# Building the row tables of a two-pass edge sort with exclusive scans, padded differences and int32 quotients

## The chip, the cores and the metric

The kernel runs on one core of one Trainium2 chip. The metric is the device time of one execution in microseconds. In the text, PE is TensorE, DVE is VectorE, ACT is ScalarE, POOL is GpSimd and SP is SyncE, as the profile names them.

## The reference

A graph has 10,000 nodes with 64 channels of 4 components each, and 640,000 edges. Each edge has a source, a destination, four spherical harmonics `Y` and four features. Each edge makes a message out of its source's row, and the messages are summed by destination:

```python
N, deg, C, L, DE = 10000, 64, 64, 1, 4
E = N * deg

def reference(x, src, dst, Y, edge_feat, w_rad, cg, w_mix):
    R = _silu(edge_feat @ w_rad)                              # (E, C)
    xs = x[src]                                                 # (E, C, M)
    tp = jnp.einsum('eci,ef,ifo->eco', xs, Y, cg)             # (E, C, M)
    msg = R[:, :, None] * tp
    agg = _segment_sum(msg.reshape(-1, C * M), dst, N).reshape(N, C, M)
    return jnp.einsum('ncm,cd->ndm', agg, w_mix)
```

Sources and destinations are random integers.

## The kernel before

The kernel sorts the edges by destination in two passes through DRAM and then works on small buckets of destinations. The edges come in three parts (32, 37 and 31%), and each part goes through all steps.

**The first pass** (`pass1`) sends the edges of a part to 18 groups of 576 destinations. Edges lie in tiles of 128; 12 tiles make a chunk. For each chunk the kernel builds rows: a row holds up to 14 edges of one group, each packed into 10 words. A one-hot matmul (line 675) moves rows to their places on the partitions, ScalarE copies them out of PSUM (line 683, tile `rt`), and GpSimd writes 128 rows at a time to DRAM by an indirect DMA with an index tile (line 687, to `grp`).

**The second pass** (`pass2`) reads one group at a time and does the same for 18 buckets of 32 destinations, with rows of up to 15 edges (line 687, to `bkt`). In this pass a row that a chunk leaves half full is carried on to the next chunk (`carry`).

**The messages** (`messages`) are made bucket by bucket. GpSimd gathers the 1 KB rows of `x` for each tile of 128 edges by an indirect DMA (line 1030, tile `xg`, seven buffers, five buckets ahead of their use). TensorE and ScalarE make the radial factors, VectorE multiplies them in (line 1083), and TensorE sums by destination into `G` (line 1098). A gather can go out when line 1098 has read the buffer that it overwrites.

**The tables** (`tables`, what the change touches) are built before a pass can route: once for up to 24 (later 14) chunks of the first pass, and once for a group of the second pass, 83 times in all: 29 in the first pass, 54 in the second. A table works on small tiles of up to 64 partitions by 18 columns, one column for each group or bucket (`B` = 18) and one partition for each chunk:

- line 401 counts the edges of each chunk and bucket; line 404 copies the totals to `n`;
- `floor` (lines 374 and 375) divides by the row's size: one instruction multiplies, adds and writes int32, a second copies the int32 tile back to float32. It gives `R`, the rows that a chunk needs, in the second pass also `f` (whole rows ahead) and a rounded `tot`;
- lines 459 to 461 turn `R` into starts: an inclusive scan, minus `R`, and a copy of the last sum into a nineteenth column (`J` = 19);
- lines 468 to 475 give each tile's place inside its chunk (`at`, and its split into two bfloat16 parts `sb`);
- lines 480 to 487 give the distance from start to place in DRAM (`dl`) and its differences from column to column (`dd`): first column, middle, and last column by an instruction each. Lines 444 to 446 do the same for a limit in the second pass's last third (`final`);
- lines 492 to 500 spread `st`, `dd` and, in the second pass, a carried row's mark `go` along a diagonal for a matmul with ones; lines 517 to 555 compare with each partition's number and give the row numbers `dest`; lines 546 to 548 take them as integers and mark rows that overflow (`fl`);
- lines 568 to 575 rank the overflowing rows (an inclusive scan, minus itself) and write the index tile for line 687.

**The order.** In the first stage, part 0 of the first pass, a scheduler orders all engines but SP. After that the orders of PE, DVE and ACT are written out by the generators: `groups` calls the message steps one by one, and between them lets the first pass of the next part and the second pass take as many steps as their due times ask for. The steps of a table stand between the steps of routing and messages on the same DVE. POOL's queue holds the gathers and the stores of both passes in one order.

Of the kernel before, what the change touches and what calls it, by code (L numbers as in the profile page):

```python
# [18 lines left out]
F = mybir.dt.float32  # L19
# [6 lines left out]
P = 128  # L26
B = 18
# [52 lines left out]
class Kernel:  # L80
# [74 lines left out]
    def consts(self):  # L155
# [47 lines left out]
        for p in (self.p1, self.p2):  # L203

            p.on = c.tile([64, B * (p.T + 1)], F, name="on" + p.key)
            nc.vector.memset(p.on, 1.0)
            nc.vector.memset(p.on.rearrange("p (b t) -> p b t", b=B)[:, :, 0:1], 0.0)
            p.cols = c.tile([64, B * (p.T + 1)], F, name="cols" + p.key)
            nc.vector.memset(p.cols, 0.0)
        self.Ub = c.tile([P, P], BF, name="Ub")  # L210
        nc.vector.tensor_copy(self.Ub, self.U)
# [157 lines left out]

    def floor(self, out, x, r, up, nm, n):  # L370

        nc = self.nc
        t = self.ph.tile([P, B], I32, name="ri", tag="ri" + nm, bufs=1)
        nc.vector.tensor_scalar(t[:n], x, 1.0 / r, ((r - 0.5) if up else 0.5) / r - 0.5, op0=OP.mult, op1=OP.add)
        nc.vector.tensor_copy(out, t[:n])

    def tables(self, ps, D, nt, rows, kov, base, cap, final=False):
# [24 lines left out]
        sums = sums[:H].rearrange("p (b t) -> p b t", b=B)  # L402
        n = w("n", B)
        nc.vector.tensor_copy(n[:H], sums[:, :, T])
# [18 lines left out]
        if ps.carry:  # L423

            f, part = w("f", B), w("part", B)
            self.floor(f[:H], pre[:H], r, False, ps.key, H)
            nc.vector.scalar_tensor_tensor(part[:H], f[:H], -float(r), pre[:H], op0=OP.mult, op1=OP.add)
            nc.vector.tensor_tensor(n[:H], n[:H], pre[:H], op=OP.add)
            self.floor(R[:H], n[:H], r, True, ps.key, H)
            nc.vector.tensor_tensor(R[:H], R[:H], f[:H], op=OP.subtract)  # L430
            self.floor(tot[:H], tot[:H], r, True, ps.key, H)
            end, sh = w("end", B), w("sh", B)
            of = lambda t, a, n=H: t[:n].rearrange("p (m a) -> p m a", a=2)[:, :, a]
            nc.vector.tensor_tensor(end[:H], off[:H], tot[:H], op=OP.add)
            till = of(end, 1)
            if final:

                lim, dlim = w("lim", B), w("dlim", J)
# [19 lines left out]
        inc, st = w("inc", B), w("st", J)  # L458
        nc.vector.tensor_tensor_scan(inc[:H], self.ones[:H, :B], R[:H], 0.0, op0=OP.mult, op1=OP.add)
        nc.vector.tensor_tensor(st[:H, :B], inc[:H], R[:H], op=OP.subtract)  # L460
        nc.vector.tensor_copy(st[:N, B:], inc[:N, B - 1:])
        if ps.carry:
            nc.vector.tensor_tensor(self.most[:N], self.most[:N], inc[:N, B - 1:], op=OP.max)

        first = w("first", B)
        at = wk.tile([P, XW], F, name="at", tag="x1" + ps.key, bufs=1)[:, :T * B]
        if ps.carry:
            nc.vector.scalar_tensor_tensor(first[:H], st[:H, :B], float(r), part[:H], op0=OP.mult, op1=OP.add)
        else:
            nc.vector.tensor_scalar(first[:H], st[:H, :B], float(r), None, op0=OP.mult)  # L470
        nc.vector.tensor_tensor(at[:H].rearrange("p (t b) -> p b t", b=B), sums[:, :, :T],
                                first[:H].unsqueeze(2).to_broadcast([H, B, T]), op=OP.add)
        sb = wk.tile([H, T * B], BF, name="sb", tag="sb" + ps.key, bufs=3)
# [3 lines left out]

        dl, dd = w("dl", B), w("dd", J)
        if final:
            nc.vector.tensor_tensor(dl[:N], off[:N], base[:N], op=OP.add)  # L480
        else:
            nc.vector.tensor_tensor(dl[:N], cap[:N], off[:N], op=OP.min)
            nc.vector.tensor_tensor(dl[:N], dl[:N], base[:N], op=OP.add)
        nc.vector.tensor_tensor(dl[:N], dl[:N], st[:N, :B], op=OP.subtract)
        nc.vector.tensor_copy(dd[:N, 0:1], dl[:N, 0:1])
        nc.vector.tensor_tensor(dd[:N, 1:B], dl[:N, 1:], dl[:N, :B - 1], op=OP.subtract)
        nc.vector.tensor_scalar(dd[:N, B:], dl[:N, B - 1:], -1.0, float(ps.none), op0=OP.mult, op1=OP.add)
        eye = self.ident[:N, :N].unsqueeze(2).to_broadcast([N, N, J])
# [5 lines left out]
        if ps.carry:  # L494

            go, bq = w("go", J), w("bq", NC * J, NC, d=BF)
            nc.vector.memset(go[:N, 0:1], 0.0)
            nc.vector.tensor_scalar(go[:N, 1:], st[:N, :B], -2.0 * P, None, op0=OP.add)
# [40 lines left out]
        nc.vector.tensor_reduce(dest[:, :N], sts[:, :N * J].rearrange("p (c j) -> p c j", j=J), axis=AX.X, op=OP.add)  # L539
        nc.vector.tensor_scalar(dest[:, :N], dest[:, :N], self.pid, None, op0=OP.add)  # L540

        if final:
            nc.vector.tensor_tensor(fl[:, :N], dest[:, :N], lm[:, :N], op=OP.is_ge)
        else:
            di = w("di", NC, d=I32)
            nc.vector.tensor_copy(di[:, :N], dest[:, :N])
            nc.vector.tensor_scalar(di[:, :N], di[:, :N], ps.stride - 1, None, op0=OP.bitwise_and)
            nc.vector.tensor_scalar(fl[:, :N], di[:, :N], float(ps.cap), None, op0=OP.is_ge)
        if ps.carry:
# [3 lines left out]
            nc.vector.tensor_tensor(fl[:, :N], fl[:, :N], un[:, :N], op=OP.is_gt)  # L553
            nc.vector.scalar_tensor_tensor(dest[:, :N], un[:, :N], float(ps.none), dest[:, :N], op0=OP.mult, op1=OP.add)
            nc.vector.tensor_scalar(tg[:, :N], tg[:, :N], 2.0 * P, None, op0=OP.add)
# [6 lines left out]
        yield  # L562
        ov, rk = w("ov", 64), w("rk", NC)
# [5 lines left out]
        nc.vector.tensor_tensor(kov, kov, rk[0:1, N - 1:N], op=OP.add)  # L569
        nc.vector.tensor_tensor(rk[:, :N], rk[:, :N], ov[:, 32:32 + N], op=OP.subtract)  # L570
        nc.vector.tensor_tensor(rk[:, :N], rk[:, :N], ov[:, :N], op=OP.add)
        nc.vector.scalar_tensor_tensor(rk[:, :N], rk[:, :N], float(ps.ovf), dest[:, :N], op0=OP.add, op1=OP.subtract)
        nc.vector.tensor_tensor(rk[:, :N], rk[:, :N], fl[:, :N], op=OP.mult)
        idx = w("idx", NC, b=3, d=I32)
        nc.vector.tensor_tensor(idx[:, :N], rk[:, :N], dest[:, :N], op=OP.add)
        self.tab[ps.key] = (sb, idx, N, tg if ps.carry else None)
# [1023 lines left out]
```

## Time and profile before

| | before |
|---|---|
| runs, us | 8428.72, 8426.91, 8418.68 |
| median, us | 8426.91 |
| profiled execution, us | 8430.4 |
| its span, us | 8428.6 |
| granted TensorE clock, mean | 0.855 |
| DVE busy, us (share of the span) | 7181.2 (85%) |
| POOL busy, us (share) | 5881.9 (70%) |
| PE busy, us (share) | 5985.1 (71%) |
| ACT busy, us (share) | 4614.3 (55%) |
| gathers of `x` (line 1030) | 5165, 957 ns each |
| stores of sorted rows (line 687) | 417 + 489, 1008 ns each |

The span reaches from the first to the last instruction of one execution. Busy time of an engine leaves out the issuing of DMAs, so for POOL, which issues indirect DMAs from first to last, the short idle time between two of them has to be counted with them. A view by stretches gives the busy time of each engine between two moments; a view of waits gives who waited for whom, how long in total, how often, and the longest.

### The profile page before, as it was taken

The page shows a single profiled execution, that of the slowest core. Times are in us where ns is not written, and L with a number is a line of the kernel's source. Part 1 is how long each engine was busy: PE and PEld are TensorE (multiplying, and loading weights), DVE is VectorE, ACT ScalarE, POOL GpSimd, SP SyncE. Part 2 cuts the span into 40 slices and gives each one's busy share as a digit, 9 for nine tenths or more (in the row PEclk, how much of TensorE's full clock was granted, in tenths as well). Part 3 has the DMA queues.
Part 4 walks back from the last instruction along what each step waited for, and adds up shares of the span by engine and source line. Part 5 has one row for each costly group of instructions (what it writes and reads, how often), then busy time and mean ns, then how long its engine had stood idle before and what let it go on. Part 6 is the DMA issues. An engine that isn't in the chain of part 4 may idle for free. (4 is left out here: it accounts for less than half of the span.)

```text
span 8428.6 us, 133579 instructions
## 1 busy us (share of the span) xinstructions
PE 5985.1 (71%) x41164; PEld 4943.4 (59%) x41164; DVE 7181.2 (85%) x14990; ACT 4614.3 (55%) x12740; POOL 5881.9 (70%) x6113
## 2 busy tenths in 40 slices
PE   5666776777767767776676676766677777778776
PEld 3334655656555656565565565555566666666666
DVE  8988999999999889988898898867787888878775
ACT  5876666666666746655565565653443443434321
POOL 1226676777767767777777777777777777777776
PEclk8977888888888879888888888887898989888888
DMA  5313343443434434444444444444455555555543
GB/s 185 112 59 96 113 117 107 118 116 112 118 110 120 119 112 129 121 122 123 120 122 124 120 119 125 116 120 121 133 147 145 145 146 145 146 148 143 146 139 114
DMA packets 691501, 1051.54 MB, mean 125 GB/s; under 512 B 268789, under 2 KB 499107, under 8 KB 690792
## 3 DMA queue, kind: packets, MB, share of 16 engines
q0 software_dynamic: 285888, 732.64, 30.5%
q1 hardware_dynamic: 402312, 301.08, 12.1%
q10 hardware_dynamic: 2592, 9.19, 0.3%
q8 instruction: 345, 5.65, 0.3%
q14 instruction: 364, 2.98, 0.1%
HBM read 841.86 MB, written 215.89 MB: 125 GB/s over the span
## 5 line engine op out<-in xcount | busy, mean ns | idle before, releaser
L1030 POOL DMA_INDIRECT xg<-in_x_dram,sidx x5165 | 4940.6, 957 | 1750.4 <-issue 1345.0
L1098 PE MATMUL G<-S,xg 128*128 128x128 f32 x20660 | 2989.8, 310 | 158.2 <-ACT Gp L1127 129.4
L1098 PEld LDWEIGHTS G<-S,xg 128*128 128x128 f32 x20660 | 2837.7, 222 | 202.2 <-ACT Gp L1127 153.3
L675 PE MATMUL pr<-X,oh 128*128 128x300 bf16 (+1 forms) x10573 | 1668.3, 312 | 548.5 <-DVE oh L657 411.4
L1083 DVE TENSOR_TENSOR xg<-xg,pre 128x1536 f32<-128x1536 f32 (+1 forms) x939 | 1516.4, 1615 | 540.3 <-DMA xg<-in_x_dram,sidx 303.3
L665 ACT ACTIVATE sq<-i,rowf 128x128 f32<-128x128 f32 x6132 | 1882.1, 391 | 11.2 <-DVE rowf L626 7.3
L641 DVE TENSOR_TENSOR X<-dv,Wt 128x1800 f32<-128x1800 f32 (+4 forms) x906 | 1741.6, 1922 | 62.1 <-PE pr L675 10.4
L675 PEld LDWEIGHTS <-oh 128*128 128x128 bf16 x10573 | 1080.1, 105 | 983.1 <-DVE oh L657 483.7
L666 ACT ACTIVATE oh<-sq,ones 128x1024 bf16<-128x1024 f32 (+3 forms) x906 | 967.1, 1067 | 27.1
L1069 DVE TENSOR_TENSOR S<-dv,pay 128x768 f32<-128x768 f32 (+1 forms) x939 | 836.7, 891 | 87.3 <-PE G L1098 29.8
L1043 PE MATMUL pre<-identb,e 128*108 128x128 bf16 x1878 | 291.2, 241 | 867.5 <-DVE xg L1083 866.6
L1043 PEld LDWEIGHTS <-e 128*108 128x108 bf16 x1878 | 236.8, 140 | 1041.1 <-issue 792.3
L1059 ACT ACTIVATE pre<-pre 128x384 f32<-128x384 f32 (+1 forms) x939 | 426.6, 454 | 716.3 <-PE pre L1056 551.0
L687 POOL DMA_INDIRECT grp<-rt,idx x417 | 420.2, 1008 | 529.0 <-ACT rt L683 196.9
L1127 ACT ACTIVATE Gp<-G 128x256 f32<-128x256 f32 x626 | 238.6, 381 | 892.0 <-PE G L1098 647.3
L687 POOL DMA_INDIRECT bkt<-rt,idx x489 | 492.7, 1008 | 224.7 <-issue 112.4
L1048 ACT ACTIVATE sT<-pre 108x256 bf16<-108x256 f32 x939 | 353.2, 376 | 527.1 <-PE pre L1043 525.2
L1143 PE MATMUL po<-wf,Gs 128*128 128x256 f32 (+2 forms) x1392 | 390.8, 443 | 184.6 <-DVE Gs L1125 184.6
L683 ACT ACTIVATE rt<-pr 128x300 bf16<-128x300 f32 (+1 forms) x906 | 358.7, 396 | 278.6 <-PE pr L678 118.5
L1143 PEld LDWEIGHTS po<-wf,Gs 128*128 128x128 f32 (+2 forms) x1392 | 282.5, 209 | 278.1 <-DVE Gs L1125 181.7
L657 DVE TENSOR_TENSOR oh<-dv,pair 128x640 bf16<-128x640 bf16 (+2 forms) x869 | 420.6, 488 | 0.3
L609 ACT ACTIVATE pc<-pp 128x432 f32<-128x432 f32 (+3 forms) x471 | 236.3, 502 | 295.5 <-DVE pos L618 227.5
(286 smaller groups left out, 6086.1 us busy)
## 6 DMA issues: line engine op xcount, KB each, us to landing
xg<-in_x_dram,sidx POOLq DMA_INDIRECT x5165
sums<-Gp SPq DMA_DIRECT2D x626, 128.0 KB
old<-sums SPq DMA_DIRECT2D x313, 256.0 KB
bkt<-z SPq DMA_DIRECT2D x26, 990.0 KB
pay<-bkt SPq DMA_DIRECT2D x68, 225.0 KB
grp<-z SPq DMA_DIRECT2D x17, 590.0 KB
Wt<-grp SPq DMA_DIRECT2D x17, 590.0 KB
ye<-in_Y_dram SPq DMA_DIRECT2D x103, 96.0 KB
```

The lines of the kernel that those rows point to most:

```text
L641: nc.vector.tensor_tensor(X[:, :m, :].rearrange("p t (s w) -> p t s w", w=W), msk.unsqueeze(3).to_broadcast([P, m, ps.r, W]), QD[c // Q][1 ...
L665: nc.scalar.activation(sq[:, u, :], self.i128, AF.Square, bias=to, scale=-1.0)
L666: nc.scalar.activation(oh[:, v:v + len(at), :], sq[:, :len(at), :], AF.Relu, bias=self.ones[:, 0:1], scale=-2.0)
L675: nc.tensor.matmul(pr[:, :2 * ps.rw], oh[:, u, :], X[:, u, :].bitcast(BF), start=(u == 0), stop=(not on and u == m - 1))
L687: st = nc.gpsimd.indirect_dma_start(out=ps.dst, out_offset=bass.IndirectOffsetOnAxis(ap=idx[:, i:i + 1], axis=0), in_=RT.pop(c), in_offset ...
L1030: nc.gpsimd.indirect_dma_start(out=xg[:, t, :], out_offset=None, in_=self.x, in_offset=bass.IndirectOffsetOnAxis(ap=si[:, u:u + 1], axis=0))
L1043: nc.tensor.matmul(pre[:KR, 256 + 128 * h:384 + 128 * h], e[:, 36 * t:36 * t + KR], self.identb, start=True, stop=True)
L1059: nc.scalar.activation(RT[k], RT[k], AF.Silu)
L1069: nc.vector.tensor_tensor(S[:, :ut], self.eq[:, :ut].unsqueeze(3).to_broadcast([P, ut, NB, 4]), pb[:, :, 1:5].unsqueeze(2).to_broadcast([P ...
L1083: nc.vector.tensor_tensor(V, V, R.unsqueeze(3).to_broadcast([P, ut, 64, 4]), op=OP.mult)
L1098: nc.tensor.matmul(G[:, h].rearrange("p n f -> p (n f)"), v[:, 32 * h:32 * h + 32, :].rearrange("p c i -> p (c i)"), s.rearrange("p n f -> ...
L1143: nc.tensor.matmul(po[:nn, :256], Gs[:, h, f].rearrange("p b n -> p (b n)")[:, :nn], self.wf[:, h, f, :], start=(h + f == 0), stop=(h + f ...
```

## The change

The tables are built with fewer instructions on DVE; the values stay the same.

- `floor` writes the int32 tile and stops there. Where a quotient is read by the next computation, that reads int32 (`f`, `Ri`, `all`); only the first pass copies it to float32, since a matmul reads it.
- The totals are no longer copied to `n`: the strided view `sums[:, :, T]` is read in place, by the matmuls too.
- Some tiles are kept for the whole program with fixed outer columns that are set once at the start: `Rx` has a zero ahead of `R`, so that an inclusive scan over 19 columns gives the exclusive starts and the total in one instruction; `dlx` and `limx` have a zero ahead and the closing value behind, so that one subtraction of shifted views gives all 19 differences; `gone` has its zero column; `ov` has a zero in column 31, ahead of the counts in columns 32 and on, so that the rank scan starts one column early and is exclusive.
- In the first pass the product `first` goes into the addition that makes `at`; in the second, outside its last third, the minimum with a constant and the addition of the base are one instruction.
- `dest` plus the partition's number is written as int32 (`di`), and the later steps read that.
- Eleven memsets at the start set the fixed columns.

```diff
@@ consts
+            p.Rx = c.tile([64, B + 1], F, name="Rx" + p.key)
+            nc.vector.memset(p.Rx, 0.0)
+            p.dlx = c.tile([32, B + 2], F, name="dlx" + p.key)
+            nc.vector.memset(p.dlx, 0.0)
+            nc.vector.memset(p.dlx[:, B + 1:], float(p.none))
+            p.ov = c.tile([P, 64], F, name="ov" + p.key)
+            nc.vector.memset(p.ov, 0.0)
...
@@ floor
-        t = self.ph.tile([P, B], I32, name="ri", tag="ri" + nm, bufs=1)
-        nc.vector.tensor_scalar(t[:n], x, 1.0 / r, ((r - 0.5) if up else 0.5) / r - 0.5, op0=OP.mult, op1=OP.add)
-        nc.vector.tensor_copy(out, t[:n])
+        self.nc.vector.tensor_scalar(t, x, 1.0 / r, ((r - 0.5) if up else 0.5) / r - 0.5, op0=OP.mult, op1=OP.add)
@@ tables
-        n = w("n", B)
-        nc.vector.tensor_copy(n[:H], sums[:, :, T])
-        R = w("R", B)
+        Ri, R = w("Ri", B, d=I32), ps.Rx[:, 1:]
         if not ps.carry:
-            self.floor(R[:H], n[:H], r, True, ps.key, H)
+            self.floor(Ri[:H], sums[:, :, T], r, True)
+            nc.vector.tensor_copy(R, Ri[:H])
...
-        cn = n if ps.carry else R
+        cn = sums[:, :, T] if ps.carry else R
...
-            self.floor(f[:H], pre[:H], r, False, ps.key, H)
+            self.floor(f[:H], pre[:H], r, False)
             nc.vector.scalar_tensor_tensor(part[:H], f[:H], -float(r), pre[:H], op0=OP.mult, op1=OP.add)
-            nc.vector.tensor_tensor(n[:H], n[:H], pre[:H], op=OP.add)
-            self.floor(R[:H], n[:H], r, True, ps.key, H)
-            nc.vector.tensor_tensor(R[:H], R[:H], f[:H], op=OP.subtract)
-            self.floor(tot[:H], tot[:H], r, True, ps.key, H)
+            nc.vector.tensor_tensor(n[:H], sums[:, :, T], pre[:H], op=OP.add)
+            self.floor(Ri[:H], n[:H], r, True)
+            nc.vector.tensor_tensor(R, Ri[:H], f[:H], op=OP.subtract)
+            self.floor(all[:H], tot[:H], r, True)
...
-                nc.vector.tensor_copy(dlim[0:1, 0:1], lim[0:1, 0:1])
-                nc.vector.tensor_tensor(dlim[0:1, 1:B], lim[0:1, 1:], lim[0:1, :B - 1], op=OP.subtract)
-                nc.vector.tensor_scalar(dlim[0:1, B:], lim[0:1, B - 1:], -1.0, 4.0 * ps.none, op0=OP.mult, op1=OP.add)
+                nc.vector.tensor_tensor(dlim[0:1], self.limx[:, 1:], self.limx[:, :J], op=OP.subtract)
...
-        nc.vector.tensor_tensor_scan(inc[:H], self.ones[:H, :B], R[:H], 0.0, op0=OP.mult, op1=OP.add)
-        nc.vector.tensor_tensor(st[:H, :B], inc[:H], R[:H], op=OP.subtract)
-        nc.vector.tensor_copy(st[:N, B:], inc[:N, B - 1:])
+        nc.vector.tensor_tensor_scan(st[:H], self.ones[:H, :J], ps.Rx, 0.0, op0=OP.mult, op1=OP.add)
...
-        else:
-            nc.vector.tensor_scalar(first[:H], st[:H, :B], float(r), None, op0=OP.mult)
-        nc.vector.tensor_tensor(at[:H].rearrange("p (t b) -> p b t", b=B), sums[:, :, :T],
-                                first[:H].unsqueeze(2).to_broadcast([H, B, T]), op=OP.add)
+        nc.vector.scalar_tensor_tensor(at[:H].rearrange("p (t b) -> p b t", b=B),
+                                       first[:H, :B].unsqueeze(2).to_broadcast([H, B, T]), k, sums[:, :, :T],
+                                       op0=OP.mult, op1=OP.add)
...
+        elif ps.carry:
+            nc.vector.scalar_tensor_tensor(dl[:N], off[:N], float(ps.cap), base[:N], op0=OP.min, op1=OP.add)
...
-        nc.vector.tensor_copy(dd[:N, 0:1], dl[:N, 0:1])
-        nc.vector.tensor_tensor(dd[:N, 1:B], dl[:N, 1:], dl[:N, :B - 1], op=OP.subtract)
-        nc.vector.tensor_scalar(dd[:N, B:], dl[:N, B - 1:], -1.0, float(ps.none), op0=OP.mult, op1=OP.add)
+        nc.vector.tensor_tensor(dd[:N], ps.dlx[:N, 1:], ps.dlx[:N, :J], op=OP.subtract)
...
-            nc.vector.memset(go[:N, 0:1], 0.0)
...
-        nc.vector.tensor_scalar(dest[:, :N], dest[:, :N], self.pid, None, op0=OP.add)
+        di = w("di", NC, d=I32)
+        nc.vector.tensor_scalar(di[:, :N], dest[:, :N], self.pid, None, op0=OP.add)
...
-            nc.vector.tensor_copy(di[:, :N], dest[:, :N])
...
-        nc.vector.tensor_tensor_scan(rk[:, :N], self.ones[:, :N], ov[:, 32:32 + N], 0.0, op0=OP.mult, op1=OP.add)
+        nc.vector.tensor_tensor_scan(rk[:, :N + 1], self.ones[:, :N + 1], ov[:, 31:32 + N], 0.0, op0=OP.mult, op1=OP.add)
...
-        nc.vector.tensor_tensor(rk[:, :N], rk[:, :N], ov[:, 32:32 + N], op=OP.subtract)
```

In the order of DVE's instructions, here is the start of a table of the second pass between two routing steps, before (the rows are line, operation, output from inputs, and shape; the scan is listed as a fused operation in such rows):

```order
L374 TENSOR_SCALAR ri<-pre 64x18
L375 CAST f<-ri 64x18
L427 SCALAR_TENSOR_TENSOR part<-f,pre 64x18
L428 TENSOR_TENSOR n<-n,pre 64x18
L374 TENSOR_SCALAR ri<-n 64x18
L375 CAST R<-ri 64x18
L430 TENSOR_TENSOR R<-R,f 64x18
L374 TENSOR_SCALAR ri<-tot 64x18
L375 CAST tot<-ri 64x18
L434 TENSOR_TENSOR end<-off,tot 64x18
```

The same piece of DVE's order with the change:

```order
L384 TENSOR_SCALAR f<-pre 64x18
L435 SCALAR_TENSOR_TENSOR part<-f,pre 64x18
L436 TENSOR_TENSOR n<-sums,pre 64x18
L384 TENSOR_SCALAR Ri<-n 64x18
L438 TENSOR_TENSOR Rxbkt<-Ri,f 64x18
L384 TENSOR_SCALAR all<-tot 64x18
L443 TENSOR_TENSOR end<-off,all 64x18
```

The three casts are gone and the rest keeps its order. Further down in the same table on DVE, the distances and their differences, before:

```order
L482 TENSOR_TENSOR dl<-bc,off 9x18
L483 TENSOR_TENSOR dl<-dl,base 9x18
L484 TENSOR_TENSOR dl<-dl,st 9x18
L485 COPY dd<-dl 9x1
L486 TENSOR_TENSOR dd<-dl 9x17
L487 TENSOR_SCALAR dd<-dl 9x1
L492 TENSOR_TENSOR bs<-ident,st 9x171
```

And with the change:

```order
L487 SCALAR_TENSOR_TENSOR dlxbkt<-off,base 9x18
L491 TENSOR_TENSOR dlxbkt<-dlxbkt,st 9x18
L492 TENSOR_TENSOR dd<-dlxbkt 9x19
L497 TENSOR_TENSOR bs<-ident,st 9x171
```

Seven rows became four. In all, DVE's order has 14842 rows before and 13972 with the change. Behind the first stage the orders of PE, DVE and ACT are the same but for the rows that are left out. In the first stage, where the scheduler sets the order, some packing steps and matmuls stand some places earlier or later. POOL's queue has a store and a few gathers exchanged in a handful of places.

More of the change, by code (lines that the diff above doesn't have):

```diff
@@ L209, in consts @@
             nc.vector.memset(p.cols, 0.0)
+            p.Rx = c.tile([64, B + 1], F, name="Rx" + p.key)
[5 more added lines that the diff above has]
+            nc.vector.memset(p.ov, 0.0)
+        self.limx = c.tile([1, B + 2], F, name="limx")
+        nc.vector.memset(self.limx, 0.0)
+        nc.vector.memset(self.limx[:, B + 1:], 4.0 * self.p2.none)
+        self.gone = c.tile([32, B + 1], F, name="gone")
+        nc.vector.memset(self.gone, 0.0)
         self.Ub = c.tile([P, P], BF, name="Ub")
@@ L368, in digits, with floor @@
             yield
-    def floor(self, out, x, r, up, nm, n):
-        nc = self.nc
-        t = self.ph.tile([P, B], I32, name="ri", tag="ri" + nm, bufs=1)
-        nc.vector.tensor_scalar(t[:n], x, 1.0 / r, ((r - 0.5) if up else 0.5) / r - 0.5, op0=OP.mult, op1=OP.add)
-        nc.vector.tensor_copy(out, t[:n])
+    def floor(self, t, x, r, up):
+        self.nc.vector.tensor_scalar(t, x, 1.0 / r, ((r - 0.5) if up else 0.5) / r - 0.5, op0=OP.mult, op1=OP.add)
     def tables(self, ps, D, nt, rows, kov, base, cap, final=False):
@@ L423, in tables @@
         if ps.carry:
-            f, part = w("f", B), w("part", B)
-            self.floor(f[:H], pre[:H], r, False, ps.key, H)
+            f, part, n, all = w("f", B, d=I32), w("part", B), w("n", B), w("all", B, d=I32)
+            self.floor(f[:H], pre[:H], r, False)
             nc.vector.scalar_tensor_tensor(part[:H], f[:H], -float(r), pre[:H], op0=OP.mult, op1=OP.add)
-            nc.vector.tensor_tensor(n[:H], n[:H], pre[:H], op=OP.add)
-            self.floor(R[:H], n[:H], r, True, ps.key, H)
-            nc.vector.tensor_tensor(R[:H], R[:H], f[:H], op=OP.subtract)
-            self.floor(tot[:H], tot[:H], r, True, ps.key, H)
+            nc.vector.tensor_tensor(n[:H], sums[:, :, T], pre[:H], op=OP.add)
+            self.floor(Ri[:H], n[:H], r, True)
+            nc.vector.tensor_tensor(R, Ri[:H], f[:H], op=OP.subtract)
+            self.floor(all[:H], tot[:H], r, True)
+            tot = all
             end, sh = w("end", B), w("sh", B)
@@ L553, in tables @@
             nc.vector.tensor_tensor(fl[:, :N], fl[:, :N], un[:, :N], op=OP.is_gt)
-            nc.vector.scalar_tensor_tensor(dest[:, :N], un[:, :N], float(ps.none), dest[:, :N], op0=OP.mult, op1=OP.add)
+            nc.vector.scalar_tensor_tensor(dest[:, :N], un[:, :N], float(ps.none), di[:, :N], op0=OP.mult, op1=OP.add)
+            di = dest
             nc.vector.tensor_scalar(tg[:, :N], tg[:, :N], 2.0 * P, None, op0=OP.add)
```

29 lines of the change are left out of this document (15 added, 14 removed).

## The prediction

> **What bounds the kernel now.** I read the busy line of the page first, then the busy time by stage, then the waits of GpSimd and of VectorE in those stages, and last the order of time around the place where GpSimd waits for the last time.
>
> ```profile
> span 8428.6 us, 133579 instructions
> PE 5985.1 (71%) x41164; PEld 4943.4 (59%) x41164; DVE 7181.2 (85%) x14990; ACT 4614.3 (55%) x12740; POOL 5881.9 (70%) x6113
> ```
>
> VectorE (DVE) has the largest share, and the change takes work from VectorE alone. But a share over the whole span mixes stages. The stages, cut at the first gather (636 us) and at the last wait of GpSimd that I find further down (3288 us):
>
> ```profile
> core 0: us, PE busy (x) PEld busy (x) DVE busy (x) ACT busy (x) POOL busy (x), PEclk, DMA share, GB/s
> 0.00:636.00 636.00, 373.69 (x2155) 221.53 (x2156) 582.64 (x1594) 462.58 (x1248) 142.76 (x156) 0.85 0.35 118
> 636.00:3288.00 2652.00, 1877.30 (x12954) 1530.35 (x12953) 2418.08 (x5133) 1707.72 (x4787) 1861.98 (x1928) 0.84 0.40 114
> 3288.00:8300.00 5012.00, 3662.50 (x25597) 3126.95 (x25595) 4123.67 (x8168) 2430.26 (x6670) 3805.53 (x3956) 0.86 0.46 132
> ```
>
> GpSimd's busy time hides a fixed step between its indirect DMAs, which the order of time shows (columns: start, duration, what, idle before it and what ended that):
>
> ```profile
> 3288.22 0.96 POOL L1030 DMA_INDIRECT xg<-in_x_dram,sidx  x1 [1.13 <-PE G L1098]
> 3289.49 0.95 POOL L1030 DMA_INDIRECT xg<-in_x_dram,sidx  x1 [0.31 <-issue]
> ```
>
> Each indirect DMA costs its 0.96 us and then some 0.305 us in which the engine waits for nothing. From 3288 to 8300 us that gives 3805.5 + 3956 x 0.305 = 5012 us, which is the whole stretch: GpSimd issues without a pause for five of the eight milliseconds, and no work saved on VectorE there can move the end. From 636 to 3288 us the same sum is 1862.0 + 1928 x 0.305 = 2450 of 2652 us, so 202 us are true waiting. What GpSimd waits for there, and what it waits for behind it:
>
> ```profile
> engine line waited for: us in total, times, longest us
> POOL xg L1030 <- PE G L1098: 117.3, 45, 10.4
> POOL xg L1030 <- PE pre L1056: 57.0, 36, 5.4
> POOL bkt L687 <- ACT rt L683: 29.7, 14, 8.2
> ...
> POOL xg L1030 <- PE G L1098: 6.7, 15, 1.6
> ```
>
> The first three rows are 636 to 3288 us, the last one, with no single wait over 1.6 us, 3288 to 8300. Up to 3288 us a gather waits until the sums (line 1098) have read the tile it will overwrite; those sums wait for VectorE's products, and VectorE itself has few waits in the same stretch:
>
> ```profile
> DVE xg L1083 <- ACT pre L1059: 22.1, 17, 3.2
> DVE xg L1083 <- DMA xg<-in_x_dram,sidx: 17.2, 8, 4.5
> ```
>
> So: VectorE paces the first 3288 us, GpSimd's queue the rest, and the time is (moment of GpSimd's last real wait) + (its remaining work at 1.27 us a piece). Only VectorE time saved before 3288 us counts.
>
> **The change part by part.** The price of a removed instruction is not its duration but the step to the start of the next one, since independent instructions overlap. One table of the second pass, in order of time:
>
> ```profile
> 1250.03 0.17 DVE L404 COPY n<-sums 64x18 f32<-64x18 f32 x1
> 1250.12 0.34 DVE L638 TENSOR_TENSOR dv<-dv,slot 128x180 f32<-128x180 f32 x1
> ...
> 1263.97 0.17 DVE L375 CAST f<-ri 64x18 f32<-64x18 int32 x1
> 1264.17 0.17 DVE L427 SCALAR_TENSOR_TENSOR part<-f,pre 64x18 f32<-64x18 f32 x1
> ...
> 1266.86 0.17 DVE L460 TENSOR_TENSOR st<-inc,R 64x18 f32<-64x18 f32 x1
> 1266.96 0.13 DVE L461 COPY st<-inc 9x1 f32<-9x1 f32 x1
> 1267.02 0.14 DVE L463 TENSOR_TENSOR most<-most,inc 9x1 f32<-9x1 f32 x1
> ...
> 1275.65 0.17 DVE L483 TENSOR_TENSOR dl<-dl,base 9x18 f32<-9x18 f32 x1
> 1275.85 0.17 DVE L484 TENSOR_TENSOR dl<-dl,st 9x18 f32<-9x18 f32 x1
> 1276.05 0.14 DVE L485 COPY dd<-dl 9x1 f32<-9x1 f32 x1
> 1276.12 0.15 DVE L486 TENSOR_TENSOR dd<-dl 9x17 f32<-9x17 f32 x1
> 1276.20 0.13 DVE L487 TENSOR_SCALAR dd<-dl 9x1 f32<-9x1 f32 x1
> 1276.27 0.32 DVE L492 TENSOR_TENSOR bs<-ident,st 9x171 bf16<-9x171 f32 x1
> ...
> 1296.52 0.17 DVE L546 CAST di<-dest 128x9 int32<-128x9 f32 x1
> 1296.73 0.17 DVE L547 TENSOR_SCALAR di<-di 128x9 int32<-128x9 int32 x1
> ```
>
> Steps of what goes in a table of the second pass: the copy of n 0.09 us; three casts behind the divisions at 0.20, 0.60; the subtraction and the copy that made the scan exclusive (lines 460 and 461) 0.10 + 0.06 = 0.16; the separate addition of the base (483) 0.20; two of the three pieces of the difference (485 and 487) 0.07 + 0.07 = 0.14; the cast of the row number (546) 0.21; the subtraction behind the rank scan (570), which the next instruction waits for as it does for the casts, 0.20. The memset of line 497 I count at nothing, since the addition beside it covers it. Sum **1.60 us** of a table's VectorE time, for 12 instructions. The last third of the second pass keeps 483 and 546 as they are but loses the same two pieces of difference once more for its limits: 1.60 - 0.20 - 0.21 + 0.14 = 1.33 us. A table of the first pass loses the copy of n (0.20, since the division waits for it), 0.16, 0.14, 0.21, 0.20, and the product that made `first` (line 470, 0.20 like the casts of that shape, since the next one waits for it): **1.11 us** for 8 instructions.
>
> The upper bound of these prices is a whole duration and the 0.03 us of idle time that stand between a cast and its reader. For the 12 instructions that is 12 durations of 0.06 to 0.17, 1.8 us, and 12 x 0.03, so 2.2 us a table, and for the 8 of the first pass 1.5 us. The rows with independent neighbours are against it: line 463 starts 0.06 us after line 461 did, which takes 0.13. The Trainium skill, "VectorE: DVE Perf Modes", section "The DRAIN you can't avoid", has the stricter rule: the next operation does not start until the pipeline of the one before is empty, so each instruction costs its whole length and their count is what is to be cut; by it a table is worth 2.2 us and not 1.6. The trace disagrees with that for the 0.06 us step, and agrees where the next instruction reads the result.
>
> What is put in their place costs nothing that I can see: the scan runs over 19 instead of 18 columns, the rank scan over one more, the difference is one instruction over 19 instead of 17 columns. New forms are integer operands and a fused operation in the place of a plain one, and the first two rows, of one size, show a fused operation on integers at the price of a plain one on floats:
>
> ```profile
> L1066 DVE TENSOR_TENSOR dv<-dv,dlc 128x192 f32<-128x192 f32 x470 | 170.6, 363 | 8.5
> L794 DVE SCALAR_TENSOR_TENSOR Wt<-ye,pkh 128x192 int32<-128x192 int32 x206 | 67.8, 362 | 2.4
> L471 DVE TENSOR_TENSOR at<-sums,first 64x216 f32<-64x216 f32 x83 | 42.8, 516 | 2.6
> L497 DVE MEMSET go<- 9x1 f32 (+3 forms) x54 | 3.2, 59 | 0.0
> ```
>
> No row shows a fused operation that mixes a broadcast with a strided operand as the new line 471 does; its bounds are 516 ns as now, and twice that, 0.5 us lost a table. I take no loss, going by those two rows. Eleven memsets come in at the start, 59 ns each as line 497: 0.7 us.
>
> How many tables lie where it counts, by the busy time of two lines in the three stretches (line 460 runs once in every table, line 497 once in every table of the second pass):
>
> ```profile
> 0.00:636.00 636.00, 1.46 (x9) 0.85 0.35 118
> 636.00:3288.00 2652.00, 5.79 (x34) 0.84 0.40 114
> 3288.00:8429.00 5141.00, 6.87 (x40) 0.86 0.46 131
> ...
> 0.00:636.00 636.00, 0.12 (x2) 0.85 0.35 118
> 636.00:3288.00 2652.00, 1.18 (x20) 0.84 0.40 114
> ```
>
> Up to 636 us: 7 x 1.11 + 2 x 1.60 = 11.0 us, less 0.7. VectorE is busy for 583 of 636 us there, and GpSimd's first gather follows it: I count 10. From 636 to 3288 us: 14 x 1.11 + 20 x 1.60 = 47.5 us. Behind that: 8 x 1.11 + 14 x 1.60 + 18 x 1.33 = 55 us, hidden by GpSimd's queue and worth **nothing**; without that cover the gain would double.
>
> Of the 47.5 us not all will reach GpSimd. VectorE's own waits in the stretch (some 110 us, of which the longest rows are quoted) take part of an advance away, and so do GpSimd's waits for an eviction to store. As bounds: all of it, or the share of GpSimd's waiting that lies with the sums, 117 of 202, which leaves 27. I take 85%, 40 us, because the other two releasers stand one step behind VectorE as well. The sum is 10 + 40 = 50 us. The profiled execution took 8430.4 us, with 1.8 us around its span; 8430.4 - 50 = 8380. The median of the runs is 3.5 us under the profiled one: **8377 us**.
>
> **The rivals.**
>
> *The advance is swallowed.* GpSimd already issues in 92% of the middle stretch, and a faster VectorE may meet gathers that have not landed; the row of 17.2 us is that wait. Then the 10 us of the first stage and at most a quarter of the rest come through: 10 to 22 us, 8405 to 8417. Against it: the gathers run five units ahead, and 117 us of waiting are on the sums.
>
> *More comes through than the steps say.* The removed casts and copies stand in chains that TensorE and ScalarE wait for, and each freed step could be worth a whole duration, the upper bound above. With 22 tables of the second pass and 21 of the first before 3288 us that is 22 x 2.2 + 21 x 1.5 = 80 us: gains of 65 to 80 us, 8347 to 8362. Against it: the overlap in the order of time. It is also what the rule of the Trainium skill named above would give.
>
> *Slower.* Before 636 us the order of all engines is not written out, and the changed program puts some packing work and some matmuls of the first batches elsewhere. Everything behind 3288 us hangs on GpSimd, so each microsecond by which the first gather comes later than 636 counts in full. GpSimd's wait for the first table of the second pass is the size of such a slip:
>
> ```profile
> 610.32 0.97 POOL L687 DMA_INDIRECT bkt<-rt,idx  x1 [32.89 <-ACT tot L420]
> ```
>
> It decides if the first gather comes later than now by more than the 40 us that the middle stretch gives: with two more waits of that size, 66 - 40 = 26 us are lost and the time is 8453. Against it: tables and chunks keep nearly the same place among each other in the new order.
>
> **How the numbers follow.** Forecast (gain of 25 to 65 us, 8362 to 8402): 0.70. Swallowed: 0.13. More: 0.11. Slower or no change by the first stage: 0.06. A change of 0.2%, 17 us, is about what a measurement of this kernel can tell; so faster takes the forecast, the larger gain and a little under half of the swallowed case, 0.87; within 0.2% the other half and a little of the last, 0.09; slower 0.04. The range holds 8 in 10 from a gain of 82 us, a little over the full price of every instruction, 8345, to one of 15 us, 8412.
>
> **What would show it right or wrong.** In the changed kernel's profile: VectorE 870 instructions fewer and some 114 us less busy or more; the first gather near 626 us; GpSimd's last wait for the sums near 3240 us; from there no true wait, and its waiting between the first gather and that point down from 202 to some 160 us; behind it VectorE's wait for gathers longer by the 55 us. The forecast is wrong if the last wait of GpSimd stays near 3288 us, if the first gather is later than now, or if line 471's new form costs far more than 516 ns.

## The result, and the profile after

The changed kernel takes 8355.0 us (median of 4 runs, 8350.1 to 8359.6) against 8425.4 us (4 runs, 8418.7 to 8428.7) of the kernel before: 70 us less, a ratio of 0.9917 with a 95% interval of 0.9900 to 0.9935. The forecast was 8377 us with a range of 8345 to 8412.

The page of the changed kernel, its span and its busy line:

```profile
span 8353.4 us, 132708 instructions
PE 5970.3 (71%) x41164; PEld 4952.7 (59%) x41164; DVE 7068.1 (85%) x14121; ACT 4611.3 (55%) x12740; POOL 5883.0 (70%) x6113
```

VectorE has 869 instructions fewer and is busy for 113.1 us less (7181.2 before); the other engines' busy time moves by 15 us or less. Of the 113 us only 75 show in the span. Where they do is seen from GpSimd's queue, whose order of gathers is the same in both kernels but for a few exchanges with stores. The times at which a gather of a given number starts, read from the order of time of both traces:

| gather number | before, us | changed, us | earlier by, us |
|---|---|---|---|
| 1st | 636.3 | 622.7 | 13.7 |
| 601st | 1674.7 | 1636.7 | 38.0 |
| 1201st | 2665.3 | 2604.3 | 61.0 |
| 1601st | 3294.5 | 3221.5 | 73.0 |
| 3001st | 5373.9 | 5299.8 | 74.2 |
| 5001st | 8147.9 | 8074.5 | 73.4 |

The advance grows until the 1601st gather and then stands still for 5 ms. A long wait of GpSimd for the sums in the kernel before, and then the first and the last wait in the changed kernel, in the order of time:

```profile
3155.65 0.98 POOL L1030 DMA_INDIRECT xg<-in_x_dram,sidx  x1 [10.36 <-PE G L1098]
...
622.66 0.99 POOL L1034 DMA_INDIRECT xg<-in_x_dram,sidx  x1 [11.15 <-DVE didx L984]
...
3083.90 0.98 POOL L1034 DMA_INDIRECT xg<-in_x_dram,sidx  x1 [10.13 <-PE G L1102]
3085.18 0.96 POOL L1034 DMA_INDIRECT xg<-in_x_dram,sidx  x1 [0.30 <-DVE dest L543]
3086.45 0.95 POOL L1034 DMA_INDIRECT xg<-in_x_dram,sidx  x1 [0.30 <-issue]
```

The last wait for the sums lies at 3084 us instead of 3288, 90 gathers earlier in the queue; the prediction expected it near 3240. The wait of 10 us is the one that stood at 3155.65 us before. The one at 3288 had been only 0.8 us longer than GpSimd's fixed step, and it is gone. Behind 3084 us GpSimd waits for nothing longer than 0.8 us up to 8230. Ahead of it, from the first gather on, its true waiting, summed as in the prediction, fell from 202 to 141 us (2461.3 us less 1763.3 of busy time and 1825 steps of 0.305). GpSimd's waits from the first gather to there, the second row being that for the sums (117.3 before), and the same view of the stretch from 3090 to 8230 us:

```profile
POOL xg L1034 <- issue: 382.7, 1256, 0.3
POOL xg L1034 <- PE G L1102: 92.8, 47, 10.1
POOL xg L1034 <- PE pre L1060: 40.9, 23, 4.6
...
POOL xg L1034 <- issue: 945.6, 3104, 0.3
POOL xg L1034 <- PE G L1102: 13.0, 41, 0.8
```

What VectorE saved in the late stretch turned into waiting. VectorE's longest waits there, before (3288 to 8300 us, two rows) and changed (3090 to 8230 us, so 128 us more; two rows):

```profile
DVE xg L1083 <- DMA xg<-in_x_dram,sidx: 271.9, 85, 11.7
DVE xg L1083 <- ACT pre L1059: 162.1, 41, 24.1
```

```profile
DVE xg L1087 <- DMA xg<-in_x_dram,sidx: 309.2, 96, 10.5
DVE xg L1087 <- ACT pre L1063: 203.0, 56, 25.5
```

The sharper account takes VectorE's order of time apart at the same gathers in each trace: the sum of the steps from one start to the next, with idle time over 0.15 us before an instruction taken out, and that idle time by itself.

| stretch | | length, us | steps, us | idle, us |
|---|---|---|---|---|
| start to 1st gather | before | 636.3 | 588.0 | 47.4 |
| | changed | 622.7 | 580.9 | 41.5 |
| 1st to 1601st gather | before | 2658.2 | 2542.9 | 115.4 |
| | changed | 2598.9 | 2484.1 | 114.4 |
| 1601st to last gather | before | 5076.7 | 4334.6 | 745.6 |
| | changed | 5074.7 | 4266.6 | 811.5 |

In the middle stretch 58.8 us of steps went and the stretch is 59.3 us shorter: all of it came through, and VectorE's idle time stayed within 1 us of what it was. In the last, 68.0 us of steps went and 65.9 us of idle time came.

### The profile page after: what moved, and what is told of

Same layout as the page of the kernel before. It is cut to its first block, busy times and chain, and to the rows that moved or that the text cites. A ratio compares the mean times of both kernels' runs of the same rounds, so it can differ in the third digit from the quotient of the medians.

```text
span 8353.4 us, 132708 instructions
## 1 busy us (share of the span) xinstructions
PE 5970.3 (71%) x41164; PEld 4952.7 (59%) x41164; DVE 7068.1 (85%) x14121; ACT 4611.3 (55%) x12740; POOL 5883.0 (70%) x6113
```

## The experiments

Each kernel was run together with the kernel before on one chip, and a batch takes whatever chip it is given. On the chips of the first result and of three later batches the kernel before takes 8422 to 8430 us. On those of four other batches it takes 10110 to 10241 us, and there the program has another bound. The runs on those chips are told with that said; the account of why they differ stands with the hardware below. Theory A is that of the prediction: VectorE paces the kernel up to GpSimd's last real wait, GpSimd's queue behind it. Rival B is that VectorE's time counts in one proportion everywhere, 70 us shown for 114 us saved. Rival C is that the memory layout or the first stage's order did it.

**Only the last third old, only the last third new.** Two kernels hold both versions of `tables`, the old one writing into the new fixed tiles:

```diff
+    def tables(self, ps, D, nt, rows, kov, base, cap, final=False):
+        how = self.tables_new if not final else self.tables_old      # the other kernel: if final
+        yield from how(ps, D, nt, rows, kov, base, cap, final)
```

> The changed kernel, but the 18 tables of the second pass's last third are built by the old instructions, 12 more each (216 in all); all other tables are new. Theory A (GpSimd's queue sets the end behind its last wait near 3100 us, so only VectorE time before it counts): these tables all lie behind that point, so nothing changes against the changed kernel, 8355 us within 8. Rival B (VectorE's saving counts in the same proportion everywhere, 70 us gained for 114 us saved): 18 x 1.33 = 24 us of VectorE come back, of which 15 us show, 8370 us.

> The opposite: only the 18 tables of the last third are new, all others are built by the old instructions. Theory A: the time of the kernel before, 8425 us within 8. Rival B: 15 us less, 8410 us. Rival C (the gain came from the other memory layout or the scheduler's other order in the first stage, not from fewer instructions): this kernel has the new fixed tiles too, so a good part of the 70 us would be kept, 8355 to 8390.

This batch's chip was of the other sort: the kernel before took 10111.7 us. The first kernel took 10058.9 us (ratio 0.9958, 0.9942 to 0.9975), the second 10110.9 us (0.9992, 0.9975 to 1.0009). So there, too, new tables in the last third alone give nothing that can be told from zero, and the rest of the tables nearly all. Rival C falls as far as it speaks of the layout: the second kernel has the new fixed tiles and no gain. It does not test the order of the first stage, since with the old instructions there the order of PE and ACT goes back to nearly that of the kernel before; but the table above puts only 13.7 us ahead of the first gather. Rival B's 15 us are not told apart from zero by these intervals, and GpSimd's queue was not without pauses on this chip; so the question went to loads of a size that shows.

**A load in the last third.** Additions of zeros, one reading the other, stand ahead of the first quotient in each of the last 18 tables:

```diff
+            self.seen += 1
+            if final:
+                for _ in range(14):
+                    nc.vector.tensor_tensor(self.zr, self.zr, self.zr, op=OP.add)
```

> The changed kernel with 14 additions of 40 x 150 zeros, one behind the other, put ahead of line 431's work in each of the 18 tables of the last third: some 0.35 us each, 4.9 us a table, 88 us of VectorE in all. Theory A: hidden behind GpSimd's queue, no change, 8355 us within 8. Rival B: 62% of 88 us show, 8410 us.

> The changed kernel itself, once more, as the measure for its variants on the chip that this batch runs on. In the batch before, the kernel before took 10112 us and TensorE's idle time was mostly put down to issue, not to a wait. Theory A on a chip like the first: 8355 us and a gain of 70 us. On a chip like that of the batch before: a gain near the 53 us that the kernel with old final tables showed there.

> The changed kernel with 88 us of additions in the 18 tables of the last third, as before. Theory A on a chip like the first: no change against the changed kernel of this batch, within 8 us. Rival B (VectorE time counts in the same proportion everywhere): 55 us slower than it. On a chip like that of the batch before: some 40 us slower, since GpSimd's queue is not the bound there.

> The same kernel with 88 us of additions in the tables of the last third, on whatever chip this batch gets. Where the kernel before takes 8.4 ms and GpSimd issues without a pause behind 3288 us, theory A: the gain of the change stays whole, 70 us under the kernel before. Rival B: 55 of the 70 us are lost, 15 us under it. Where the kernel before takes 10.1 ms, as in the last two batches, nothing new: 10100 us, some 50 us above the changed kernel.

The first two runs fell on chips of the other sort: 10099.8 us against 10111.7 (0.9988, 0.9973 to 1.0002), and in the next batch 10100.5 us where the changed kernel itself took 10051.0 and the kernel before 10110.4 (0.9990, 0.9973 to 1.0008, and 0.9942, 0.9923 to 0.9962). There the load costs about 50 of its 88 us. The third run had a chip like the first one: **8365.5 us** against 8429.8 (0.9926, 0.9910 to 0.9943), a gain of 64 us where the changed kernel had 70. In its trace, the group of the additions, and between 3090 and 8230 us VectorE's longest wait and GpSimd's row for the sums:

```profile
L437 DVE TENSOR_TENSOR zr<-zr 40x150 f32<-40x150 f32 x252 | 77.4, 307 | 8.1
...
DVE xg L1092 <- DMA xg<-in_x_dram,sidx: 248.6, 84, 12.3
POOL xg L1039 <- PE G L1107: 12.7, 40, 0.8
```

77 us of busy time more (84 us of steps), 73 us of idle time less between the 1601st gather and the last (811.5 to 738.1), and the stretch is 13 us longer. Rival B would have it 55 us longer. The 13 us are no wait of GpSimd: from the 1601st to the 5001st gather no pause between two of its indirect DMAs is over 0.32 us, but the DMAs themselves took longer. The gathers of that stretch in the changed kernel and in this one:

```profile
L1034 POOL DMA_INDIRECT xg<-in_x_dram,sidx x3400 | 3245.3, 955 | 1035.8 <-issue 888.6 <-DMA xg<-in_x_dram,sidx 25.6 <-DMA bkt<-rt,idx 24.7
L1039 POOL DMA_INDIRECT xg<-in_x_dram,sidx x3400 | 3259.8, 959 | 1036.4 <-issue 892.3 <-DMA xg<-in_x_dram,sidx 28.7 <-DMA bkt<-rt,idx 21.3
```

The kernel with the load early (below), which has none here, is also 5.5 us longer in that stretch, so a part of the 13 us is spread between runs; whether VectorE's load slows GpSimd's DMAs was not tested. By the gains, 64 us against 70, the late load costs some 6 us, less than the two intervals can tell apart. So on this sort of chip theory A holds for the last third; on the other sort it doesn't, and there GpSimd has waits to the end.

**The same load early.** The changed kernel with 12 such additions in the first 22 tables of the second pass (`if self.seen <= 22`, `range(12)`).

> The changed kernel with 12 such additions in each of the first 22 tables of the second pass, all ahead of GpSimd's last wait: 4.2 us a table, 92 us of VectorE. Theory A with full pass-through: all of it shows, 8447 us. Theory A with the 85% that the prediction took for the share that reaches GpSimd: 8433 us. Rival B: 62%, 8412 us.

> The changed kernel with 12 additions of 0.35 us in each of the first 22 tables of the second pass, 92 us of VectorE ahead of GpSimd's last wait, on a chip where the kernel before takes 8.4 ms. Theory A with full pass-through: 92 us above the changed kernel, 22 us above the kernel before, 8447 us. With the 85% that the prediction took: 78 us above the changed kernel, 8433 us. Rival B (62% everywhere): 8412 us, under the kernel before.

On the chip of the first batch it took 10130.0 us (1.0035, 1.0022 to 1.0047 of the kernel before). On a chip like that of the first result: **8436.5 us** against 8429.9 (1.0008, 0.9999 to 1.0018). The group of the additions, and GpSimd's last wait:

```profile
L437 DVE TENSOR_TENSOR zr<-zr 40x150 f32<-40x150 f32 x264 | 81.1, 307 | 8.4
...
3284.96 0.97 POOL L1039 DMA_INDIRECT xg<-in_x_dram,sidx  x1 [1.88 <-PE G L1107]
```

The load's steps are 88 us (8.0 up to the first gather, 79.9 in the middle stretch), and the last wait is back at 3285 us, where the kernel before had it. Against the 70 us that the change gained, this kernel lies 77 us above the changed one, 87% of the load. In the two traces the 1601st gather is 70 us later (3291.2 against 3221.5), 79% of the load, and the rest comes behind it, where GpSimd's DMAs take longer. In the middle stretch, 63.2 us longer, idle time fell from 114.4 to 103.1 us and so took 11 of the 80 us; the other instructions' steps are 5 us fewer. By the gains, the same amount of VectorE work that costs some 6 us late costs 77 early. Rival B's 8412 us is out.

**What one removed instruction frees.** The step behind the running count (line 569 before, 574 now) had shrunk by more than the prediction had priced. One width was changed:

```diff
-        nc.vector.tensor_tensor(rk[:, :N], rk[:, :N], ov[:, :N], op=OP.add)
+        nc.vector.tensor_tensor(rk[:, :N + 1], rk[:, :N + 1], ov[:, :N + 1], op=OP.add)
```

> The changed kernel with one width changed: the addition behind the rank scan (line 575) runs over N + 1 columns instead of N, so that it writes over the total in column N that line 574 has just read, as the subtraction of the kernel before did. Theory: the step from line 574 to the next start is 0.08 us in the changed kernel and was 0.18 in the kernel before because the next instruction had to wait until the total was read; then it is 0.18 again here. Rival (the step fell because the ranks are summed by one instruction fewer): it stays 0.08.

The order of time in the kernel before, in the changed kernel, and with the wider addition:

```profile
1318.20 0.15 DVE L569 TENSOR_TENSOR kov<-kov,rk 1x1 f32<-1x1 f32 x1
1318.38 0.17 DVE L570 TENSOR_TENSOR rk<-rk,ov 128x9 f32<-128x9 f32 x1
1318.58 0.17 DVE L571 TENSOR_TENSOR rk<-rk,ov 128x9 f32<-128x9 f32 x1
```

```profile
1290.00 0.15 DVE L574 TENSOR_TENSOR kov<-kov,rk 1x1 f32<-1x1 f32 x1
1290.08 0.15 DVE L575 TENSOR_TENSOR rk<-rk,ovbkt 128x9 f32<-128x9 f32 x1
1290.26 0.18 DVE L576 SCALAR_TENSOR_TENSOR rk<-rk,dest 128x9 f32<-128x9 f32 x1
```

```profile
1397.02 0.15 DVE L574 TENSOR_TENSOR kov<-kov,rk 1x1 f32<-1x1 f32 x1
1397.20 0.17 DVE L575 TENSOR_TENSOR rk<-rk,ovbkt 128x10 f32<-128x10 f32 x1
1397.41 0.17 DVE L576 SCALAR_TENSOR_TENSOR rk<-rk,dest 128x9 f32<-128x9 f32 x1
```

The median step over all 83 tables is 182 ns before, 77 in the changed kernel, 182 with the wider addition. So the wait of 0.1 us hangs on the write over the total that the instruction ahead reads, and the exclusive scan took it away because the total now lies in a column that nobody writes over. The traces' records of semaphores (the counters by which one instruction tells another that it is done) show what holds it: in the kernel before and with the wider addition the second instruction waits, in all 83 tables, for VectorE's own semaphore, which the first raises; in the changed kernel it waits for none. So it is a wait that the program itself asks for; whether the engine would hold the second instruction without it is not shown. Over the whole trace of the kernel before, where VectorE was otherwise not idle, an instruction that waits only for that semaphore, raised by the one ahead, starts 34 ns after the one ahead has ended (median of 6981), and one that waits for none starts 82 ns before that end (median of 4114). (The run with the wider addition was on a chip of the other sort, 10237.7 us; the durations in the rows shown differ by 0.02 us at most.)

**A version that takes more from VectorE early.** If VectorE's early time counts in full, moving one-hot tiles to ScalarE should gain as well:

```diff
-            self.p1.act = self.p2.act = 7
+            self.p1.act = self.p2.act = 8
```

> The changed kernel with eight of a chunk's twelve one-hot tiles made on ScalarE instead of seven behind the first stage, so VectorE makes four (some 0.09 us less a chunk) and ScalarE 0.39 us more. On a chip where the kernel before takes 8.4 ms, theory A: some 330 chunks lie before GpSimd's last wait, so up to 30 us less than the changed kernel, 8325 to 8345 us, as long as ScalarE, 67% busy there, does not become the bound. Rival: ScalarE, which also empties PSUM for TensorE, delays that, and the time is 8360 us or more.

> The same kernel with eight one-hot tiles on ScalarE, on whatever chip this batch gets. Where the kernel before takes 8.4 ms, theory A: up to 30 us less than the changed kernel, a gain of 80 to 100 us against the kernel before. Rival (ScalarE delays TensorE): a gain of 65 us or less. Where the kernel before takes more than 10 ms: no gain, as in the batch before.

> Once more the kernel with eight one-hot tiles on ScalarE, in the hope of a chip where the kernel before takes 8.4 ms. Theory A: a gain of 80 to 100 us against the kernel before, up to 30 us more than the changed kernel has. Rival (ScalarE delays TensorE): 65 us or less. On a chip above 10 ms: no gain, as twice before.

Twice on chips of the other sort it showed no gain over the kernel before (10246.2 against 10240.7, 1.0001 from 0.9984 to 1.0019; 10225.6 against 10221.7, 1.0002 from 0.9991 to 1.0014). On a chip like the first: **8355.6 us** against 8421.8 (0.9924, 0.9908 to 0.9941), a gain of 66 us, at the rival's edge and no better than the changed kernel. From 636 to 3288 us, the changed kernel and this one (columns as in the prediction's view by stages):

```profile
636.00:3288.00 2652.00, 1898.59 (x13320) 1552.00 (x13319) 2418.42 (x4847) 1742.06 (x4884) 1908.08 (x1976) 0.85 0.41 117
```

```profile
636.00:3288.00 2652.00, 1895.81 (x13314) 1545.17 (x13312) 2397.47 (x4846) 1866.61 (x5211) 1910.42 (x1977) 0.86 0.41 117
```

VectorE's steps between the first and the 1601st gather fell by 22.8 us, to 2461.3, and its idle time rose by 20.0, to 134.4: the stretch is 2.7 us shorter. ScalarE is busy for 125 us more. VectorE's wait for ScalarE's `pre` in that stretch is 33.2 us where it was 23.8, its wait for TensorE's `pr` 11.8 where it was 4.1, and TensorE waits 37.0 us for ScalarE's one-hot tiles where it waited 19.1. That fits the rival, that ScalarE delays the others; which of these waits took the 20 us is not shown apart. No version here beats the changed kernel.

## Why the prediction was right, and where it was off

**The bound and the place** were right: VectorE up to GpSimd's last wait, GpSimd's queue behind it, nothing for the 40 tables of the late stretch. The still-standing 73 to 74 us from the 1601st gather on, the load that costs some 6 us late and 77 us early, and VectorE's idle time that takes up 66 of 68 us late show it.

Of the 23 us by which the first 1601 gathers gained more than the 50 us of the sum, 11 lie in the prices, some 8 in the share and 4 in the first stage.

**The share that comes through** was off. The prediction took 85% of the middle stretch, 40 of 47.5 us, and feared VectorE's and GpSimd's own waits. The runs show 59.3 us of time for 58.8 us of steps; VectorE's idle time stayed at 114 us. The 85% do fit the load that was added (87%) and fit worse still for work moved to ScalarE (12%). A reading that fits is that freed time counts as long as it meets no other engine's work, but no run here tests that for the tables' instructions by themselves.

**The price of a table** was the other mis-sized term: 47.5 us were priced for the 34 tables of the middle stretch, and 59 were freed. By lines, from the steps in both traces:

| part | priced, us | measured, us |
|---|---|---|
| copy of the totals `n` | 4.6 | 9.6 |
| casts behind the divisions | 12.0 | 13.2 |
| exclusive scan | 5.4 | 5.6 |
| addition of the base | 4.0 | 4.2 |
| difference in one piece | 4.8 | 4.1 |
| product `first` | 2.8 | 3.4 |
| cast of the row number | 7.1 | 7.7 |
| subtraction behind the rank scan | 6.8 | 11.3 |

Two rows make 9.5 of the 11.6 us between the two columns. The rank scan's 0.1 us a table is the wait shown above. The copy of `n` was priced at 0.09 us from a single table. Fourteen of the 20 second-pass tables of the stretch have the products (line 1083) behind that copy, with a step of 0.27 us, and six the masks or spots, with 0.09; why the step is longer ahead of the products was not tested. And the scan ahead of it lost its reader. Its rows before (the copy's own row, at 1250.03, stands in the prediction) and in the changed kernel:

```profile
1249.37 0.63 DVE L401 TENSOR_TENSOR_SCAN sums<-onbkt,colsbkt 64x234 f32<-64x234 f32 x1
```

```profile
1222.87 0.63 DVE L410 TENSOR_TENSOR_SCAN sums<-onbkt,colsbkt 64x234 f32<-64x234 f32 x1
1223.42 0.32 DVE L642 TENSOR_TENSOR dv<-dv,slot 128x180 f32<-128x180 f32 x1
```

The step behind the scan was 0.66 us with a reader next and is 0.55 us with unrelated work next. So a removed instruction frees its own step and the wait that it caused on the one ahead, and the prediction counted only the first. The rule of the Trainium skill that was weighed there ("VectorE: DVE Perf Modes", "The DRAIN you can't avoid") would have given an estimated 80 us up to the last wait, against 66 us of steps that went (73 us of time). The same section adds that a next operation which is not held starts earlier, which the prediction left out. The trace agrees with the rule where the next instruction waits for the semaphore of the one ahead (a start 34 ns behind its end), and not elsewhere (82 ns ahead of it).

**The new forms** cost next to nothing, as taken: the fused addition with a broadcast (line 475) has a step of 0.553 us against 0.552 of line 471, and the integer operands show in no step of the tables by more than 0.01 us.

**The first stage**: 10 us were taken, 13.7 came. Its steps fell by 7.1 us, less than the 11 worked out, and the rest is idle time, 47.4 to 41.5 us. That idle time depends on the scheduler's order, and no run here tells apart how much of it is the change's.

**The rivals.** "Swallowed" and "slower" did not come; "more comes through than the steps say" named 8347 to 8362, and the time fell inside that band. Its reason, that a freed step is worth more than the step itself, was the right one for `n` and the rank scan, though not by a whole duration for every instruction, and wrong for the differences and the base. The forecast's own band, 8362 to 8402, missed by 7 us.

## What to carry to other kernels

Cut the span where the queue that never pauses has its last real wait: engine time ahead of that point can count in full (59 of 59 us for the removed instructions here, 70 to 77 of 88 for a load), behind it hardly at all, and a load put in on each side measures both. Price a removed instruction by the step in every place where it stands, and add the waits that it puts on its neighbours, for a result that it reads or a value that it writes over; one example out of one place is not enough. Work that is moved to another engine is not work removed, even if that engine is busy for two thirds of the time: here 3 of 23 us came through.

## What the runs showed of the hardware

The same program ran in about 8.43 ms on some chips and in 10.1 to 10.2 ms on others, each time steady over a whole batch. The changed kernel on the first sort and on the other, its cores view and one stretch in the middle:

```profile
core 0: 8353.4 us, clock 0.853
...
4000.00:5000.00 1000.00, 709.61 (x5048) 601.09 (x5047) 860.87 (x1557) 590.82 (x1630) 759.60 (x790) 0.85 0.42 122
```

```profile
core 0: 10070.8 us, clock 0.798
...
4000.00:5000.00 1000.00, 666.43 (x4174) 535.57 (x4174) 720.76 (x1330) 498.57 (x1370) 633.75 (x661) 0.79 0.35 102
```

The records of the granted clock hold half speed for 41% of their time there and for 30% on the first sort. But a lower clock is not all that the order of time shows. On the other sort TensorE often starts something only every 0.7 us with nothing to wait for: 790 steps of 0.65 to 0.75 us stand between its records in this trace, 89 in that on the first sort. In the rows below, weight loads of the routing matmuls stand 1.4 us apart, with one matmul recorded between each two. And three engines start within 0.23 us after long waits for a signal whose sender the trace does not tell ("remote"; 982 such waits in this trace, none on the first sort), 8 us after the last matmul of the sums recorded ahead of them has ended. It looks as if ends were told late; that is a reading, not a measurement.

```profile
4519.83 0.10 PEld L679 LDWEIGHTS <-oh 128*128 128x128 bf16 x1 [1.35 <-issue]
4521.23 0.10 PEld L679 LDWEIGHTS <-oh 128*128 128x128 bf16 x1 [1.30 <-issue]
4522.64 0.11 PEld L679 LDWEIGHTS <-oh 128*128 128x128 bf16 x2 [1.32 <-issue]
...
4524.20 0.38 ACT L1131 ACTIVATE Gp<-G 128x256 f32<-128x256 f32 x1 [6.64 <-remote]
4524.20 0.96 DVE L1073 TENSOR_TENSOR S<-dv,pay 128x768 f32<-128x768 f32 x1 [7.46 <-remote]
4524.43 0.94 POOL L1034 DMA_INDIRECT xg<-in_x_dram,sidx  x1 [2.64 <-remote]
```

There GpSimd waits for the sums to the end, so its queue is not without pause, and the load in the last third costs about half of itself. From 7000 to 9900 us, the changed kernel on that chip:

```profile
POOL xg L1034 <- PE G L1102: 458.0, 102, 13.1
POOL xg L1034 <- issue: 441.1, 1430, 5.3
```

What makes TensorE issue late on those chips was not found: the transfers of instructions take about as long on both (a median of 1.08 us there and 1.01 us on the first sort for 16 KB), and no run here sets the clock apart from the rest. The gain of the change on that sort of chip is 0.6%, 10051.0 against 10110.4 us.
